# The last batch's u transposed by transfers, batch 0's state kept in PSUM, and a new order: a gated linear attention with a token and channel mixer on one core

## The chip, the cores and the metric

The kernel runs on one core of one Trainium2 chip, in one launch. The metric is the device time of that core in microseconds, as the median of several runs; lower is better. The core has a matrix engine (TensorE, PE in the profile), a vector engine (VectorE, DVE), an activation engine (ScalarE, ACT), a general engine (GpSimd, POOL) and a queue engine (SyncE, SP). Each works through its own list of instructions in order and waits on semaphores for what the others make.

## The reference

The inputs are q, k, v and f_logit, each of shape (4 batches, 8 heads, 768 steps, 48), and four weights. A gated linear attention is followed by a mixer over tokens and one over channels:

```python
def _attn_ref(q, k, v, f_logit):
    f = 1.0 / (1.0 + np.exp(-f_logit))
    state = zeros((B, H, D, D))
    for t in range(S):
        state = f[:, :, t, :, None] * state + einsum('bhd,bhe->bhde', k[:, :, t], v[:, :, t])
        y[:, :, t] = einsum('bhd,bhde->bhe', q[:, :, t], state)
    return y

def _moe_ref(x, w_tok1, w_tok2, w_ch1, w_ch2):      # x: (4, 768, 384), the heads side by side
    xt = x.transpose(0, 2, 1)
    h = np.maximum(xt @ w_tok1, 0.0) @ w_tok2       # w_tok1 (768, 256), w_tok2 (256, 768)
    u = x + h.transpose(0, 2, 1)
    h2 = np.maximum(u @ w_ch1, 0.0) @ w_ch2         # w_ch1 (384, 1536), w_ch2 (1536, 384)
    return u + h2
```

## The kernel before

**Tiling.** Each batch's 768 steps are cut into six chunks of 128. Within a chunk the recurrence is computed as a masked product of q and k times v, and between chunks a state is carried.

**The stages of a chunk.** `gates` makes the logarithm of the gate (ACT) and its low half (DVE or POOL). `sums_and_turns` adds these up along the chunk on PE, takes exponentials on ACT (`GG`), scales q and k with them on DVE (`qk`, L586) and transposes both: on PE with a copy out of PSUM (L603) for batches 0 to 2, and by a transposing transfer issued from SP (L593) for batch 3 (`TURNED = 3`). `attention` computes the scores (L504) and the chunk's part of the state (L520, `parts`) on PE. `rest` masks the scores (`AmT`, L640), updates the state, copies it in two halves into the bf16 tile `state_bd`, and computes the chunk's output y on PE from `state_bd` of the chunk before (L671) and from the masked scores (L678).

**The state.** It lies in SBUF. For the first chunk it is the part scaled by the decay `glast` (L649); for each later chunk the part, which stands in a PSUM bank of its own, is first added to it (`tsum`, L652) and the sum is scaled (L654).

**The mixer.** Two products over the tokens (`tok1` L708, `tok2` L724) give u; u is cast to bf16 (`u_bf`) and transposed in two halves of three tiles (nine 128x128 blocks each) on PE (L765), with three copies by DVE or ACT per half (`uT`). The first channel product (`ch1`, L783) is 24 groups of three matmuls per batch, whose results go through a relu on ACT or DVE into `zT`; the second (`ch2`, L802) is six groups of 12 matmuls, whose results are added to u on DVE (L808) and written out from SP (L812). The code has a branch already that transposes u by two transfers; `U_TURNED` lists the batches that take it and is empty.

**The order.** The kernel first collects all its work as operations of a `Plan`: for each the engines that may do it, a rank, what it needs and makes, a PSUM bank, and a duration. `Plan.order` then runs a list schedule over these: it takes the operation that can start first by its durations (plus a lag of its own), and on a tie the one of lowest rank. The instructions are issued in the order that comes out, so the plan's durations and landing times decide each engine's order, while the chip decides the times. `SHIFTS` holds, for some of the operations by number, a rank and a lag that override the written ones. `LATE` adds some hundred nanoseconds to the plan's landing time of batch 0's loads. Where the plan sees PE idle in the first 25.5 us, it puts filler matmuls on the constant tile `steady` (L849).

**The loads.** Batch 0's q, k, v come one chunk at a time from POOL's queue, f_logit from SP's; then the weights and the later batches from POOL's.

Of the kernel before, what the change touches and what calls it, by code (L numbers as in the profile page):

```python
# [19 lines left out]
U_TURNED = ()  # L20
TURNED = 3
SHIFTS = (
# [860 lines left out]
```

## Time and profile before

| what | us |
|---|---|
| median of 3 runs | 178.74 |
| lowest and highest run | 178.43, 179.81 |
| span of the profiled execution | 176.5 |
| PE busy in it | 165.9 (94%) |
| DVE, ACT, POOL busy in it | 127.1, 120.3, 100.9 |

The span is the time from the first to the last instruction of the one profiled execution. No time of that execution as a run is listed beside its span; the runs' median lies 2.24 us above the span. Busy time of PE counts its filler matmuls, and the durations of matmuls overlap, because they are pipelined. In the profile's rows a line number is that of the kernel before; several operations can share a line where a helper issues them (`copy_on` is L459 on ACT, L461 on DVE, L463 on POOL). In a row of the timeline the first number is the start, the second the time taken, x the number of instructions merged; brackets give the idle time before it and what ended it.

### The profile page before, as it was taken

How to read it: one execution, taken by the hardware profiler on the slowest of the kernel's cores; microseconds unless marked ns; L12 is line 12 of the kernel's file. 1: busy time of each engine (PE TensorE's matmuls, PEld its weight loads, DVE VectorE, ACT ScalarE, POOL GpSimd, SP SyncE). 2: the span in 40 equal slices, each digit the busy share in tenths (PEclk: the TensorE clock that was granted, in tenths of full speed). 3: DMA queues.
4: the chain of work that ended last, by engine and by line, in shares of the span. 5: the costliest groups of instructions: out<-in, count | busy, mean ns of one | idle time of the engine just before them, and what ended most of it. 6: DMA issues, size and time to landing. Idle time of an engine off the chain costs nothing.

```text
span 176.5 us, 4283 instructions
## 1 busy us (share of the span) xinstructions
PE 165.9 (94%) x1649; PEld 104.7 (59%) x1653; DVE 127.1 (72%) x286; ACT 120.3 (68%) x273; POOL 100.9 (57%) x136
## 2 busy tenths in 40 slices
PE   6898898899999999799999999999999999999991
PEld 2355565556666676466567666675667666655660
DVE  6469886996888999988959995899485566401321
ACT  4688895879599676999897789847844332795000
POOL 7999568994499978987994997602011120000000
PEclk9999999999999999999999999999999999999998
DMA  7999999999999999999998999943902011200232
GB/s 101 131 159 161 138 169 180 214 151 204 186 168 141 225 233 97 199 116 92 113 160 45 121 193 147 202 104 59 123 9 85 2 45 49 90 0 0 87 106 78
DMA packets 97796, 21.54 MB, mean 122 GB/s; under 512 B 90512, under 2 KB 96912, under 8 KB 97776
## 3 DMA queue, kind: packets, MB, share of 16 engines
q0 software_dynamic: 79440, 13.77, 98.0%
q1 hardware_dynamic: 18336, 7.51, 19.0%
q8 instruction: 13, 0.21, 0.5%
q14 instruction: 7, 0.06, 0.1%
HBM read 25.17 MB, written 4.72 MB: 169 GB/s over the span
## 4 chain that ended last, share of the span: by engine, by line
PE 51%; ACT 5%; DVE 3%; issue 0%
PE ps L802 20%; PE ps L783 17%; PE ps L708 2%; PE ps L724 2%; PE ps L504 2%; PE ps L765 1%; ACT u_bf L459 1%; DVE AmT L640 1%; PE ps L678 1%; PE ps L603 1%; PE ps L520 1%; PE ps L671 1%; PE ps L554 1%; DVE x_nat L808 1%; PE ps L555 1%; ACT ends L574 1%
## 5 line engine op out<-in xcount | busy, mean ns | idle before, releaser
L802 PE MATMUL ps<-w_ch,zT 128*128 128x384 bf16 (+2 forms) x300 | 52.4, 320 | 0.0
L783 PE MATMUL ps<-uT,w_ch 128*128 128x384 bf16 x288 | 51.9, 326 | 0.4 <-ACT zT L468 0.4
L468 ACT ACTIVATE zT<-ps 128x384 bf16<-128x384 f32 x70 | 33.3, 491 | 14.8 <-PE ps L783 12.5
L802 PEld LDWEIGHTS <-zT 128*128 128x128 bf16 x300 | 27.7, 98 | 16.6
L783 PEld LDWEIGHTS <-w_ch 128*128 128x128 bf16 x288 | 27.2, 98 | 17.4 <-issue 0.9
L640 DVE TENSOR_TENSOR AmT<-ps,tri_bf 128x512 bf16<-128x512 f32 x46 | 29.9, 682 | 3.6 <-PE ps L504 3.4
L401 POOL DMA_DIRECT2D v_sb<-in_v_dram x24 | 22.4, 933 | 4.4 <-DMA w_ch<-in_moe_w_ch_dram 4.4
L808 DVE TENSOR_TENSOR x_nat<-x_nat,ps 128x384 f32<-128x384 f32 (+2 forms) x25 | 13.3, 535 | 16.1 <-PE ps L802 15.9
L401 POOL DMA_DIRECT2D qk_sb<-in_k_dram x24 | 22.7, 947 | 0.8 <-POOLq L867 0.8
L401 POOL DMA_DIRECT2D qk_sb<-in_q_dram x24 | 22.7, 946 | 0.0
L470 DVE TENSOR_SCALAR zT<-ps 128x384 bf16<-128x384 f32 x26 | 13.8, 550 | 8.4 <-PE ps L783 8.4
L586 DVE TENSOR_TENSOR qk<-qk_sb,GG 128x768 bf16<-128x768 bf16 (+1 forms) x30 | 14.2, 479 | 4.7 <-ACT GG L565 2.2
L463 POOL CAST state_bd<-state 48x192 bf16<-48x192 f32 x13 | 4.4, 342 | 21.8 <-DVE state L654 11.4
L401 POOL DMA_DIRECT2D f_sb<-in_f_logit_dram x18 | 16.6, 947 | 0.2
L479 ACT ACTIVATE f_sb<-f_sb 128x384 f32<-128x384 f32 x24 | 12.4, 516 | 3.5 <-DMA f_sb<-in_f_logit_dram 3.3
L849 PE MATMUL ps<-steady 128*128 128x512 bf16 x37 | 11.6, 431 | 1.6 <-DVE steady L433 1.5
L459 ACT ACTIVATE state_bd<-state 48x192 bf16<-48x192 f32 x27 | 9.7, 360 | 4.4 <-DVE state L654 3.5
L565 ACT ACTIVATE GG<-ps 128x384 bf16<-128x384 f32 x24 | 11.6, 487 | 1.6 <-PE ps L555 1.4
L603 PE MATMUL ps<-ident,qk 128*128 128x128 bf16 x144 | 11.4, 220 | 1.0 <-DVE qk L586 0.9
L567 ACT ACTIVATE GG<-ps 128x384 bf16<-128x384 f32 x24 | 11.3, 493 | 0.6 <-PE ps L555 0.3
L603 PEld LDWEIGHTS <-qk 128*128 128x128 bf16 x144 | 8.8, 98 | 4.6 <-DVE qk L586 3.1
L740 DVE TENSOR_TENSOR x_nat<-x_nat,ps 128x384 f32<-128x384 f32 x21 | 10.5, 546 | 0.8 <-PE ps L724 0.7
(75 smaller groups left out, 245.6 us busy)
## 6 DMA issues: line engine op xcount, KB each, us to landing
out_dram<-x_nat SPq DMA_DIRECT2D x23, 192.0 KB, 3.1
f_sb<-in_f_logit_dram POOLq DMA_DIRECT2D x18, 192.0 KB, 5.4
qk_sb<-in_k_dram POOLq DMA_DIRECT2D x24, 96.0 KB, 5.2
qk_sb<-in_q_dram POOLq DMA_DIRECT2D x24, 96.0 KB, 5.3
v_sb<-in_v_dram POOLq DMA_DIRECT2D x24, 96.0 KB, 5.2
f_sb<-in_f_logit_dram SPq DMA_DIRECT2D x6, 192.0 KB, 4.3
w_ch<-in_moe_w_ch_dram POOLq DMA_DIRECT2D x2, 576.0 KB, 7.2
w_ch<-in_moe_w_ch_dram POOLq DMA_DIRECT2D x1, 1152.0 KB, 11.3
```

The source lines that it names most:

```text
L401: lambda eng=eng, into=into, of=of: eng.dma_start(out=into, in_=of),
L468: nc.scalar.activation(out_, in_, AF.Relu, bias=0.0, scale=1.0)
L470: nc.vector.tensor_scalar(out_, in_, 0.0, None, ALU.max)
L479: add(ACT, r, lambda: nc.scalar.activation(fb, fb, AF.Exp, bias=0.0, scale=-1.0), make=[key], kind=el)
L565: add(ACT, r, lambda: nc.scalar.activation(G[i], sview(), AF.Exp, bias=0.0, scale=-1.0), make=[("G", i)], bank=p_s, kind=el)
L586: add(DVE, r, lambda n=n: nc.vector.tensor_tensor(qk[i4][:, n, :, 0:D], qk_sb[nb][:, n, :, c, :], GG[i][:, n], ALU.mult), need=[(x, nb, c) ...
L603: nc.tensor.transpose(to[:, o + hp, :], blk(src)[:, hp, :], ident)
L640: add(DVE, r, lambda half=half, made=made: nc.vector.tensor_tensor(half, made(), tb4, ALU.mult), need=["tri_bf"], make=[("AmT", i, p)], ba ...
L783: nc.tensor.matmul(banks[pm.at][:, 0:384], lhsT=w[:, kt, c0:c0 + 128], rhs=uT[:, th, :, kt, :], start=(kt == 0), stop=(kt == 2))
L802: nc.tensor.matmul(banks[pm.at][:, 0:n1 - n0], lhsT=zT[:, kt, tt * 128:(tt + 1) * 128], rhs=w_ch2[:, kt, n0:n1], start=(kt == 0), stop=(kt ...
L808: add(DVE, rank("ch2", tt), lambda un=un, pm=pm, n=n1 - n0: nc.vector.tensor_tensor(un, un, banks[pm.at][:, 0:n], ALU.add), make=[("x_nat" ...
L849: nc.tensor.matmul(banks[NBANK - 1], lhsT=steady[:, 0:128], rhs=steady, start=True, stop=True)
```

## The change

It has four parts.

1. `U_TURNED = (3,)`: the last batch's u is transposed by two transfers issued from SP, each of which waits for three tiles of `u_bf` and writes one half of `uT`. The 18 PE transposes and six copies of that batch go.
2. Batch 0's state stays in one PSUM bank, `p_st`. The matmuls of `parts` add onto it, DVE scales it in place, and the two copies to `state_bd` read it there, on ACT or DVE. `tsum` and the SBUF state are used from batch 1 on only. `parts` of batch 0 is now an operation of its own, no longer tied to the scores in front of it.
3. The plan takes the landings of batch 0's q, k, v and of the two token weights from a table of times (`SLOTS`), and those of f_logit from a table of delays (`HELD`), in place of `LATE`.
4. `SHIFTS` is a new table, which gives nearly all of the 1125 operations a rank and a lag.

```diff
-U_TURNED = ()
+U_TURNED = (3,)
 TURNED = 3
 SHIFTS = (
-    (8,-60,3900), (38,-50,3700), (42,-50,3800), (48,-50,3800), (53,50,3400), (55,300,6300), (85,0,2500),
...
+    (0,-34375,1200), (1,-34428,700), (2,-34357,0), (3,-34277,0), (4,-34359,0), (5,-32498,2200),
...
-LATE = {("f", 0, 1): 900, ("f", 0, 2): 200, ("f", 0, 3): 600, ("f", 0, 4): 700, ("f", 0, 5): 900,
...
+SLOTS = (4700, 6200, 7400, 8250, 10000, 11000, 11750, 12850, 13900, 14650, 15850, 16950, 17800, 18550, 19250,
+         19950, 20650, 21500, 23700, 26450)
+HELD = (0, 4400, 4450, 4200, 4600, 5400)
...
-                if len(op.kind) > 5:
-                    op.end += op.kind[5]
+                if e == POOL and size and op.kind[4] > 8000 or slot in (18, 19) and size and e == POOL:
+                    op.end = max(t + 3500, SLOTS[slot])
+                    wire = op.end - 1100
+                    slot += 1
+                elif op.kind[5:] and op.kind[5]:
+                    op.end = t + op.kind[5]
...
+    p_st = Bank()
+
     def attention(b, cs, due):
...
-        p_d, live = Bank(), [c for c in cs if c < NCH - 1]
+        p_d, live = p_st if b == 0 else Bank(), [c for c in cs if c < NCH - 1]
...
-        if live:
-            chain = add(PE, due(b, cs[0]), lambda: None, need=need, bank=p_d, kind=("mm", 1),
-                        room=1 if b == 0 else 3)
+        if live and b:
+            chain = add(PE, due(b, cs[0]), lambda: None, need=need, bank=p_d, kind=("mm", 1), room=3)
...
-                                     rhs=v_sb[nb][:, h, c, :], start=True, stop=True)
-
-        if live:
+                                     rhs=v_sb[nb][:, h, c, :], start=b > 0 or (c == 0 and hp == 0), stop=True,
+                                     skip_group_check=b == 0)
+
+        if live and b == 0:
+            add(PE, due(b, cs[0]), parts, need=[("kh", cs[0] % 4), ("v", nb, cs[0])], make=["sums"], bank=p_d,
+                kind=("mm", 345, 238))
+        elif live:
...
-            if c == 0:
+            if b == 0:
+                add(DVE, r, lambda: nc.vector.tensor_tensor(dg(), dg(), gb, ALU.mult),
+                    need=[("glast", g4)], make=["sums"], bank=p_d, kind=small)
+            elif c == 0:
...
-                op = add(((POOL, ACT) if c > 2 else ACT, ACT, (ACT, POOL), POOL)[b], r, None, need=["state", ("sbd", i)], make=[("sbd", i, cols.start)],
-                         kind=("el", HP * D, False, 1))
+                op = add(((ACT, DVE), ACT, (ACT, POOL), POOL)[b], r, None,
+                         need=["state" if b else "sums", ("sbd", i)], make=[("sbd", i, cols.start)],
+                         kind=("el", HP * D, b == 0, 1), bank=None if b else p_d)
                 op.fn = lambda op=op, rows=rows, cols=cols: copy_on(
-                    op.engine, state_bd[i][rows, :, cols], state[rows])
+                    op.engine, state_bd[i][rows, :, cols], state[rows] if b else dg()[rows])
```

The branch that part 1 turns on is in the kernel before (`op` durations of 1500, 5000 and 1900 ns are the plan's: SP's own time, the time to landing, and the share of the transfers' engines):

```python
        for th in range(2 if b in U_TURNED else 0):
            add(SP, rank("ut", 3 * th), lambda th=th: nc.sync.dma_start_transpose(
                out=uT[:, th].rearrange("p tt d t -> p (tt d) t"),
                in_=u_bf[:, 3 * th:3 * th + 3, :].rearrange("t tt n -> t (tt n)")),
                need=[("u_bf", 3 * th + j) for j in range(3)],
                make=[("uT", 3 * th + j, d) for j in range(3) for d in range(3)], kind=("fix", 1500, 5000, 1900))
```

More of the change, by code (lines that the diff above doesn't have):

```diff
@@ L208, in order @@
         banks = [0.0] * (NBANK - 1) + [until]
-        wire = 0.0
+        wire, slot = 0.0, 0
         landed: list = []
@@ L402, in load @@
                 make=[(n, i, j) for j in range(cs.start, cs.stop)],
-                kind=("load", 430 if engine == SP else 900,
-                      128 * H, size, 8000 if b else 20000, LATE.get((n, b, c), 0)))
+                kind=("load", 430 if engine == SP else 900, 128 * H, size, 8000 if b else 20000,
+                      *(() if b else (HELD[c] if engine == SP else -1,))))
     def load_w(name, dst, src, size):
@@ L509, in attention @@
             chain = add(PE, due(b, cs[0]), lambda c=c, k=k: scores(c % 4, heads[k]), need=need, bank=heads[k][1],
-                        kind=("mm", own if live else own + 107, own), tail_of=chain)
+                        kind=("mm", own if live and b else own + 107, own), tail_of=chain)
             plan.maker[heads[k][0]] = chain
```

234 rows, old and new, of tables (LATE, SHIFTS) are left out of this document.

## The prediction

> **What bounds the kernel now.** I read the stretches of the span first, cut where the first and the last channel matmuls begin and end, then the chain that ended last, then the timeline of the first 35 us and of the last batch, and the waits.
>
> ```profile
> core 0: us, PE busy (x) PEld busy (x) DVE busy (x) ACT busy (x) POOL busy (x), PEclk, DMA share, GB/s
> 0.00:34.16 34.16, 29.08 (x336) 16.88 (x341) 25.98 (x75) 25.00 (x60) 28.91 (x46) 1.00 1.62 157
> 34.16:146.85 112.69, 110.73 (x1140) 71.69 (x1138) 92.98 (x195) 84.25 (x191) 71.94 (x91) 1.00 1.31 127
> 146.85:172.94 26.09, 26.05 (x179) 16.18 (x176) 7.55 (x18) 11.08 (x23) 0.00 (x0) 1.00 0.17 62
> 172.94:176.50 3.56, 0.00 (x0) 0.00 (x0) 0.55 (x1) 0.00 (x0) 0.00 (x0) 0.86 0.15 55
> ...
> L849 PE MATMUL ps<-steady 128*128 128x512 bf16 x37 | 11.6, 431 | 1.6 <-DVE steady L433 1.5
> ```
>
> From 34.16, where batch 0's first channel matmul starts, to 172.94, PE is idle for 112.69 - 110.73 = 1.96 us and 26.09 - 26.05 = 0.04 us, at full granted clock. So 138.8 us of the 176.5 are bought with PE work alone: there, only a removed matmul or one of those 2.0 us can shorten the end. The first 34.16 us are different: PE is idle for 34.16 - 29.08 = 5.08 us, and 11.6 us of what counts as busy are 37 filler matmuls on a constant tile (the durations overlap). There the landings of batch 0 and the latency behind them set the pace. The last 3.56 us are one addition and the last output transfer; no edit touches them.
>
> ```profile
> 145.54 0.50 PE ps L765 x9
> ...
> 150.92 0.50 PE ps L765 x9
> 151.42 9.75 PE ps L783 x60
> ...
> 172.94 0.55 DVE x_nat L808
> ```
>
> This is the chain of waits near its end: nothing but PE from the last batch's transposes on. The two groups of nine transposes of u are the ones the change takes away.
>
> **Part 1, the last batch's u.** Removed: 18 PE transposes, 2 x 0.50 = 1.00 us of the chain, and six DVE copies of 0.346 us. Added: two transposing transfers on SP, each of 9 blocks of 128x128, and PE's wait for them. The trace has their like: the six transposes of q and k of this batch, 8 blocks each.
>
> ```profile
> L593 SPq DMA_TRANSPOSE qkT<-qk x6: 1232/1257/1351, 105.4 to 125.3; - x6
> DMA to landing us min/median/max: 3.1/3.7/5.5
> ...
> 105.39 1.35 SPq L593 DMA_TRANSPOSE qkT<-qk  x1
> qkT<-qk SPq DMA_TRANSPOSE x1, 5.5
> ...
> L461 DVE COPY uT<-ps x6: 345/346/357, 145.7 to 152.4; 128x384 bf16<-128x384 bf16 x6
> ...
> SPq L812 <- DVE x_nat L808: 53.1, 18, 11.9
> ...
> 145.19 0.51 POOL L463 CAST u_bf<-x_nat 128x384 bf16<-128x384 f32 x1 [0.89 <-DVE x_nat L740]
> 145.38 0.67 PE L765 MATMUL ps<-ident,u_bf 128*128 128x128 bf16 x9
> ...
> 146.20 0.81 PE L802 MATMUL ps<-w_ch,zT 128*128 128x384 bf16 x4
> 146.85 1.63 PE L783 MATMUL ps<-uT,w_ch 128*128 128x384 bf16 x9
> 148.31 1.46 PE L802 MATMUL ps<-w_ch,zT 128*128 128x384 bf16 x8
> 149.62 0.65 PE L783 MATMUL ps<-uT,w_ch 128*128 128x384 bf16 x3
> 150.10 0.81 PE L802 MATMUL ps<-w_ch,zT 128*128 128x384 bf16 x4
> 150.75 0.67 PE L765 MATMUL ps<-ident,u_bf 128*128 128x128 bf16 x9
> ```
>
> A transfer waits for three casts of u; the third ends at 145.19 + 0.51 = 145.70. Scaled by 9/8, the landing takes 3.7 x 9/8 = 4.2 us (estimate; from 3.1 and 5.5: 3.5 to 6.2). The first channel matmul of the batch would then start at 149.9, not 146.85: 3.05 us later. What can fill this on PE is batch 2's second channel product, of which 12 matmuls still stand behind 146.85 (8 + 4, 1.30 + 0.65 = 1.95 us in the chain). So with all else as it is, 1.1 us would be exposed and the 1.0 us saved would be given back; with the slowest landing 3.1 us would be exposed (5.05 - 1.95), net +2.1; with more of batch 2 held back nothing is, net -1.0. The second half is cheap: its transfer lands behind 36 channel matmuls of the first half, 36 x 0.1625 = 5.9 us of cover (9.75 us / 60 each). More filler exists: four more of these matmuls run at 146.20, and others earlier, between the token products, whose waits they cover. The diff gives the transfer 5000 ns in the plan, more than the 4.2 I expect, so the new order should hold back enough. I take -0.8 (0.2 us left exposed), with -1.0 and +2.1 as ends. On SP the two issues of 1.26 us are queued among the output transfers, and an output that waits (18 times for a sum on DVE, up to 11.9 us) holds a transpose placed behind it; what is queued behind the transposes is outputs alone, which nobody waits for until the end. The freed 2.1 us of DVE lie beside PE work and I count them as nothing: DVE is busy 7.55 of 26.09 us in that stretch.
>
> A rule speaks against this part: the Trainium skill, "VectorE: DVE Perf Modes", section "The three transpose paths", gives a 128x128 bf16 block 390 ns on TensorE and 1309 ns by the transposing transfer, and its rules say to use TensorE. By that price nine blocks would take 11.8 us (estimate) and the part would lose some 7 us. The trace does not agree: eight blocks landed 3.1 to 5.5 us after issue, not 10.5, so they are not done one after another at that price.
>
> **Part 2, batch 0's state in PSUM.** Removed: four additions (tsum) on DVE. Kept: the scaling, now in place in the bank, and two copies per chunk, now read from PSUM, by ACT or DVE; POOL can no longer take the two that it had.
>
> ```profile
> L652 DVE TENSOR_TENSOR tsum<-state,ps x4: 341/341/347, 14.7 to 26.0; 128x192 f32<-128x192 f32 x4
> L649 DVE TENSOR_TENSOR state<-ps,glast x1: 348/348/348, 13.3 to 13.3; 128x192 f32<-128x192 f32 x1
> L459 ACT ACTIVATE state_bd<-state x8: 347/360/363, 13.7 to 27.3; 48x192 bf16<-48x192 f32 x8
> L463 POOL CAST state_bd<-state x2: 336/340/345, 23.8 to 24.2; 48x192 bf16<-48x192 f32 x2
> ...
> 15.00:20.00 5.00, 3.90 (x56) 2.35 (x57) 4.39 (x13) 4.63 (x13) 4.79 (x7) 1.00 2.39 152
> 20.00:25.00 5.00, 4.80 (x82) 3.46 (x81) 4.60 (x14) 4.30 (x12) 2.25 (x5) 1.00 1.72 173
> ```
>
> DVE loses 4 x 0.341 = 1.36 us, ACT and DVE gain about 2 x 0.35 = 0.70 us; together -0.66 us on two engines that are 4.4 to 4.6 of 5 us busy just where the scan runs. A copy from PSUM of this shape isn't in the trace; the scaling of the same 192 columns reads PSUM in 0.348 and the ACT copy reads SBUF in 0.360, so I take no difference. There is a new wait: a chunk's part of the state may be added only after the scaling and both copies of the chunk before (0.35 + 2 x 0.36 = 1.07 us when both are on ACT), and in PE's order the transposes and scores placed behind it wait too; DVE and ACT wait for those. Before, the part went to a bank of its own and the adding waited on DVE. The chain per chunk is as long as it was (matmul, scaling, copies instead of addition, scaling, copies). One bank of the eight is held through the scan, instead of one from a chunk's scores to its addition. Ends: -1.36 (all of the removed work on the path) and +1.07 (the new wait once, not covered). I take -0.2, a third of the -0.66, since half of those engines' work there waits on landings.
>
> **Part 3, the landings in the plan and the order.** These move work only. How much the start can give is bounded by when batch 0's last data land.
>
> ```profile
> 1.32 1.05 POOL L401 DMA_DIRECT2D qk_sb<-in_k_dram  x1 [0.80 <-POOLq L867]
> qk_sb<-in_k_dram POOLq DMA_DIRECT2D x1, 96.0 KB, 4.6
> ...
> 16.04 0.96 POOL L401 DMA_DIRECT2D qk_sb<-in_k_dram  x1
> qk_sb<-in_k_dram POOLq DMA_DIRECT2D x1, 96.0 KB, 6.3
> 16.91 0.96 POOL L401 DMA_DIRECT2D qk_sb<-in_q_dram  x1
> qk_sb<-in_q_dram POOLq DMA_DIRECT2D x1, 96.0 KB, 5.8
> 24.29 0.73 DVE L586 TENSOR_TENSOR qk<-qk_sb,GG 128x384 bf16<-128x384 bf16 x2
> ...
> 19.78 0.70 POOL L408 DMA_DIRECT2D w_tok<-in_moe_w_tok_dram  x1 [0.21 <-issue]
> w_tok<-in_moe_w_tok_dram POOLq DMA_DIRECT2D x1, 384.0 KB, 7.8
> 30.33 2.11 PE L724 MATMUL ps<-h1T,w_tok 128*128 128x384 bf16 x12 [0.49 <-DVE h1T L470]
> ```
>
> The last chunk's k lands at 16.04 + 6.3 = 22.34 and its q at 16.91 + 5.8 = 22.71, and they are first used at 24.29 and 24.66: 1.95 us of slack. The second token weight lands at 19.78 + 7.8 = 27.58 and is used at 30.33: 2.75 us. The queue of loads is not reordered, so the start can give at most 1.95 us. Against the whole of it: the diff's table puts this k at 19.95 and q at 20.65 of the plan's clock, 2.39 and 2.06 us ahead of the trace, while the first k (4.70 in the table, landed at 1.32 + 4.6 = 5.92) is 1.22 ahead; so the plan counts on the last chunk about 1 us too early and the engines, which run in order, will wait there. I take -0.8, with -1.95 and +1.0 (the wait with no gain) as ends. In the middle a search can win back at most the 1.96 us of idle time and can lose any of it again; I take -0.4, with -1.96 and +4 as ends (twice the present idle time more; the least certain number here).
>
> **The sum.** -0.8 - 0.2 - 0.8 - 0.4 = -2.2 us on the profiled execution's span of 176.5 us: 174.3. The runs' median, 178.74, is 2.24 us above that span; I carry this over, since nothing around the span changes: 176.5 us, 1.2% faster. A change of about 1% (1.8 us) is what a measurement of this kernel tells from none.
>
> **The rivals.**
> - All parts pay in full: -1.0 for u, -1.95 for the start, -1.9 in the middle: 173.9 us. For it: PE is idle or filling for much of the first 34 us. Against: the plan's early landings and DVE and ACT near full there.
> - The transposes are hidden anyway, or paid back: 1.1 us exposed for 1.0 saved, the start and the middle unchanged, since the order was near PE's work already: 178.8 us. For it: the 12 matmuls of cover as they stand, and 98% of busy PE in the middle. Against: a plan that knows the 5 us.
> - The last batch's transposed u comes late (the slower side). Place: PE before the first channel matmul of batch 3. The transfer takes 6.2 us from the slowest row, or stands on SP behind an output that waits. Price: 3.1 exposed - 1.0 saved = 2.1 us; with nothing gained elsewhere 180.8 us. It decides from a stall of about 1.0 us on, where the part begins to lose. Against: the 5.5 us landing was of the transfer issued at 105.39, beside loads; from 146.85 on the queues move 62 GB/s against the 127 of the stretch before.
> - The newly searched order stalls PE in the middle. Place: between 34 and 147 us, where one early instruction in PE's queue holds all behind it. Price: 4 us more idle, less the 0.8 and 1.0 gained for u and the start (with part 2): 180.9 us. Against: the old order lost only 1.96 us by the same method.
>
> **How the numbers follow.** The forecast gets 0.44, with a range of its own from 175.3 to 177.4 (parts 1 and 3 shifted by about 1 us either way); three quarters of it lie below 176.95, the 1% bound. In full 0.12; paid back 0.20 (0.17 within 1%, 0.03 above); late u 0.12; stalls in the middle 0.12. Faster by over 1%: 0.33 + 0.12 = 0.45. Within 1%: 0.11 + 0.17 = 0.28. Slower: 0.03 + 0.12 + 0.12 = 0.27. The range reaches from the full payment to the two slower cases, 173.7 to 181.0; less than 0.2 is left outside, mostly above.
>
> **What would show it.** Right: no PE transposes of u in the last batch, and less than 0.5 us of PE idle before its first channel matmul; first channel matmul of batch 0 about 1 us earlier than 34.16; PE idle from there to the last matmul not above 2 us; no tsum before 35 us. Wrong: the transfers landing more than 5 us after issue or issued late behind an output; the last chunk's q and k still first used at 24 us; more than 3 us of PE idle between the first and the last channel matmul.

## The result and the profile after

The kernel after takes 176.42 us (median of 4 runs, 175.93 to 176.76) against 178.76 us for the kernel before beside it: a ratio of 0.9856, 95% interval 0.9828 to 0.9885. The same kernel in a second comparison gave 176.47 us and 0.9857 [0.9811, 0.9903]. The forecast was 176.5.

The profiled execution of after spans 174.9 us; before's spanned 176.5. That pair understates the change: each run lists its span, and their medians are 174.55 (after) and 176.8 to 177.3 (before, in three comparisons), so the profile of before was one of its shortest executions and that of after one of its longer ones. In all these runs the time is some 1.7 us above the span.

The stretches of the span of after, cut at the same places as those of before (first channel matmul of batch 0, first channel matmul of the last batch, end of the last matmul):

```profile
core 0: us, PE busy (x) PEld busy (x) DVE busy (x) ACT busy (x) POOL busy (x), PEclk, DMA share, GB/s
0.00:34.34 34.34, 27.88 (x328) 16.03 (x329) 26.15 (x74) 24.39 (x59) 27.98 (x43) 1.00 1.63 156
34.34:148.23 113.89, 111.90 (x1143) 72.38 (x1141) 90.03 (x184) 87.25 (x196) 74.84 (x96) 1.00 1.31 130
148.23:171.82 23.59, 23.59 (x158) 14.61 (x155) 9.61 (x19) 6.68 (x14) 0.00 (x0) 1.00 0.18 68
171.82:174.90 3.08, 0.01 (x1) 0.00 (x0) 0.30 (x2) 0.00 (x0) 0.00 (x0) 1.00 0.38 131
```

From the first channel matmul to the last matmul PE is busy 111.90 + 23.59 = 135.49 us, against 136.78 before: 1.29 us less work. Its idle time there is 1.99 us, against 2.00: nothing won back, nothing lost. The start is no shorter in these two profiles (34.34 against 34.16). One profile of each is a weak measure of it, though: in the four kernels below that share before's start (b_dma_u, b_dma_cov, b_tail, b_tail2) the first channel matmul stands at 34.27 to 34.78, in three that share after's (a_again, a_pe_u, a_u23) at 33.51 to 34.64. The tail, which no part of the change was meant to touch, is 3.08 us instead of 3.56.

The last batch's u, in the timelines of PE and of SP of after:

```profile
144.01 0.49 PE L840 MATMUL ps<-h1T,w_tok 128*128 128x384 bf16 x2
144.33 4.06 PE L918 MATMUL ps<-w_ch,zT 128*128 128x384 bf16 x24
148.23 1.95 PE L899 MATMUL ps<-uT,w_ch 128*128 128x384 bf16 x11
```

```profile
143.08 3.95 SPq L870 DMA_TRANSPOSE uT<-u_bf  x2
```

and in the view of the tile `uT`, its two rows on the transfers (ns; the second in us):

```profile
L870 SPq DMA_TRANSPOSE uT<-u_bf x2: 1290/1292/1295, 143.1 to 145.7; - x2
DMA to landing us min/median/max: 2.8/2.9/2.9
```

The first transfer is issued at 143.08 and has landed by 143.08 + 2.9 = 146.0. PE has 24 matmuls of batch 2's second channel product to do from 144.33 on, twice the 12 that stood there before, and goes over to the first channel matmul at 148.23 without a wait: 2.2 us of cover to spare.

The start of after, from the timeline of PE (brackets: idle time before, and what ended it):

```profile
30.03 2.11 PE L840 MATMUL ps<-h1T,w_tok 128*128 128x384 bf16 x12 [0.49 <-DVE h1T L578]
31.97 0.28 PE L881 MATMUL ps<-ident,u_bf 128*128 128x128 bf16 x2
32.72 0.56 PE L881 MATMUL ps<-ident,u_bf 128*128 128x128 bf16 x7 [0.47 <-ACT u_bf L567]
33.83 0.68 PE L881 MATMUL ps<-ident,u_bf 128*128 128x128 bf16 x9 [0.54 <-DVE u_bf L856]
34.34 0.98 PE L899 MATMUL ps<-uT,w_ch 128*128 128x384 bf16 x5
```

### The profile page after: what moved, and what is told of

It is laid out like the page before. It is cut to its first block, busy times and chain, and to the rows that moved or that the text cites. A ratio compares the mean times of both kernels' runs of the same rounds, so it can differ in the third digit from the quotient of the medians.

```text
span 174.9 us, 4237 instructions
## 1 busy us (share of the span) xinstructions
PE 163.4 (93%) x1624; PEld 103.0 (59%) x1624; DVE 126.1 (72%) x278; ACT 118.3 (68%) x268; POOL 102.8 (59%) x139
## 4 chain that ended last, share of the span: by engine, by line
PE 73%; ACT 8%; POOL 6%; DVE 4%; DMA 4%; issue 2%; DVEq 0%; POOLq 0%
PE ps L899 27%; PE ps L918 25%; DMA qk_sb<-in_q_dram 4%; POOL qk_sb L509 3%; PE ps L840 3%; PE ps L715 3%; PE ps L824 3%; PE ps L612 3%; PE ps L794 2%; PE ps L787 2%; ACT u_bf L567 2%; PE ps L666 2%; PE ps L667 1%; POOL v_sb L509 1%; ACT state_bd L567 1%
## 5 line engine op out<-in xcount | busy, mean ns | idle before, releaser
L918 PE MATMUL ps<-w_ch,zT 128*128 128x384 bf16 (+2 forms) x300 | 51.6, 320 | 0.2 <-ACT zT L576 0.2
L899 PE MATMUL ps<-uT,w_ch 128*128 128x384 bf16 x288 | 50.8, 326 | 0.0
L576 ACT ACTIVATE zT<-ps 128x384 bf16<-128x384 f32 x69 | 32.8, 490 | 15.4 <-PE ps L899 15.2
L571 POOL CAST state_bd<-state 48x192 bf16<-48x192 f32 x14 | 5.1, 363 | 12.3 <-DVE state L769 10.6
L677 ACT ACTIVATE GG<-ps 128x384 bf16<-128x384 f32 x24 | 11.6, 486 | 1.1 <-PE ps L667 0.9
L567 ACT ACTIVATE x_bf<-ps 128x384 bf16<-128x384 f32 x16 | 7.8, 489 | 5.7 <-PE ps L794 4.9
L965 PE MATMUL ps<-steady 128*128 128x512 bf16 x30 | 9.8, 444 | 1.5 <-DVE steady L541 1.5
```

The lines of the kernel that those rows point to most:

```text
L567: nc.scalar.activation(out_, in_, AF.Copy, bias=0.0, scale=1.0)
L576: nc.scalar.activation(out_, in_, AF.Relu, bias=0.0, scale=1.0)
L899: nc.tensor.matmul(banks[pm.at][:, 0:384], lhsT=w[:, kt, c0:c0 + 128], rhs=uT[:, th, :, kt, :], start=(kt == 0), stop=(kt == 2))
L918: nc.tensor.matmul(banks[pm.at][:, 0:n1 - n0], lhsT=zT[:, kt, tt * 128:(tt + 1) * 128], rhs=w_ch2[:, kt, n0:n1], start=(kt == 0), stop=(kt ...
```

## The experiments

### Undoing one part at a time

Three kernels keep after's order of all other instructions. In a_pe_u the last batch's u is transposed on PE again; in a_sbuf batch 0's state lies in SBUF again, with its four additions and with copies that read SBUF; a_order has both undone, so that the order and the plan alone remain of the change.

```diff
 # a_pe_u: at the place of each of the two transfers' plan operations
+    nc.tensor.transpose(to[:, j * 128:(j + 1) * 128], u_bf[:, 3 * th + j, d * 128:(d + 1) * 128], ident)   # nine
+    nc.vector.tensor_copy(uT[:, th, :, d, :], ...)                                                         # three
 # a_sbuf: in batch 0, in place of the scaling in PSUM
-    nc.vector.tensor_tensor(dg(), dg(), gb, ALU.mult)
+    if c:
+        nc.vector.tensor_tensor(tsum, state, dg(), ALU.add)
+    nc.vector.tensor_tensor(state, tsum if c else dg(), gb, ALU.mult)
```

> The changed kernel, its order kept, with the last batch's u turned on PE again: 18 transposes and six copies put back where the casts of u are ready, the two transfers left out. Theory (PE is the bound from the first channel matmul on, and the transfers are hidden): PE has 1.0 us more to do, so 177.4 us against 176.4, and the last batch's first channel matmul starts about 1.0 us later than 148.2. Rival (the gain is the order's alone, the transposes lay in idle time): 176.4. Rival (each transpose costs its row's 0.219 us): 18 x 0.219 = 3.9 us more, 180.3.

> The changed kernel, its order kept, with batch 0's state in SBUF again: each scaling is preceded by the addition (tsum), and the copies read SBUF. Theory (the start is set by when the data land, and DVE and ACT have slack there): 176.4 to 176.6. Rival (DVE is the bound of the start): four additions of 0.34 us more on the path, 177.8.

> Both edits undone in the changed kernel's order: u on PE and the state in SBUF, so that against the kernel before only the order and the plan's landings are changed. Theory (the transposes give 1.0, the order the rest): 177.4 to 177.6, 1.2 us below the kernel before. Rival (the order gives nothing): 178.7. Rival (the order gives all): 176.4.

| kernel | median us | ratio to before | first channel matmul | PE busy from there | tail |
|---|---|---|---|---|---|
| before, beside them | 178.62 | 1 | 34.16 | 136.77 | 3.61 |
| a_order | 177.88 | 0.9968 [0.9948, 0.9987] | 34.47 | 136.45 | 3.20 |
| a_pe_u | 177.19 | 0.9921 [0.9891, 0.9951] | 34.56 | 136.44 | 3.22 |
| a_sbuf | 176.91 | 0.9899 [0.9874, 0.9924] | 34.54 | 135.60 | 3.05 |
| after | 176.42 | 0.9856 [0.9828, 0.9885] | 34.34 | 135.49 | 3.08 |

(The last three columns are from one profiled execution each; those of before and after are the ones shown above, measured to the end of the last matmul, 172.89 in before. The profile of a_pe_u is of its slowest run.) Beside each other on one chip, the order and the plan are worth 178.62 - 177.88 = 0.7 us, the transfers 177.88 - 176.91 = 1.0 us and the state in PSUM 177.88 - 177.19 = 0.7 us. The sum, 2.4, is the 2.3 that the whole change gained, so the parts add up. Each is uncertain by about 0.5 us. Of the expectations, that of a_pe_u came out (177.19 for 177.4); a_order lies 0.3 us above its 177.4 to 177.6, and a_sbuf between its theory (176.4 to 176.6) and its rival (177.8). The gain of the transfers can be seen in the profile: PE's work after the first channel matmul falls by 136.44 - 135.49 = 0.95 us. That of the state cannot be seen there (136.45 and 136.44, 135.60 and 135.49), so it should come from the start. These profiles do not show it there: after's start ends between 33.51 and 34.64 from one execution to the next, which is more than the gain.

### The transfers alone, in before's order

In b_dma_u the kernel before keeps its order, and only the 18 transposes and six copies of the last batch give way to two transfers behind the third cast of each half. b_dma_cov also moves the 12 matmuls of batch 2's second channel product ahead of the first channel matmul of batch 3.

```diff
+    nc.sync.dma_start_transpose(out=uT[:, th]..., in_=u_bf[:, 3 * th:3 * th + 3, :]...)   # behind the third cast of a half
 # b_dma_cov too:
+    ahead((888, 889, 884), 1107)     # three groups of four ch2 matmuls ahead of the first ch1 group
```

> The kernel before, its order kept, with the last batch's u turned by two transfers, each issued where the third cast of its half is; the 18 PE transposes and their copies are left out. No other work is moved, so the matmuls that would cover the transfer stay behind the first channel matmul. Theory (the transfer's landing decides where its cover is missing): the third cast of the first half ends at 145.2, the landing takes 2.9 us as in the changed kernel, so PE waits from about 146.3 to 148.3, 1.9 us, and has 1.0 us less to do: 179.5, 0.9 above the kernel before. Rival (the prediction's 4.2 us landing): 3.1 us of waiting, 180.7. Rival (transfers are free wherever they stand): 177.6.

> As the run before, but 12 matmuls of batch 2's second channel product (1.95 us) are moved ahead of the last batch's first channel matmul. Theory (what counts is the work held back, not the transfer): the wait shrinks from 1.9 us to 0.1 and the run is about 1.0 us below the kernel before, 177.6 to 177.8. Rival (4.2 us landing): 1.2 us of waiting stay, 178.8.

b_dma_u took 180.31 us, ratio 1.0104 [1.0065, 1.0142]; b_dma_cov 178.83 us, 0.9977 [0.9945, 1.0008]; before beside them 179.12. PE's timeline of b_dma_u, and the landing in its view of `uT`:

```profile
145.81 0.81 PE L802 MATMUL ps<-w_ch,zT 128*128 128x384 bf16 x4
149.07 1.62 PE L783 MATMUL ps<-uT,w_ch 128*128 128x384 bf16 x9 [2.45 <-DMA uT<-u_bf]
```

```profile
DMA to landing us min/median/max: 2.8/3.0/3.2
```

The same two views of b_dma_cov:

```profile
146.15 2.76 PE L802 MATMUL ps<-w_ch,zT 128*128 128x384 bf16 x16
149.19 3.07 PE L783 MATMUL ps<-uT,w_ch 128*128 128x384 bf16 x16 [0.29 <-DMA uT<-u_bf]
```

```profile
DMA to landing us min/median/max: 2.8/2.9/3.0
```

So the same edit loses 1.2 us where only four matmuls stand behind the transfer. Where 12 more do, it comes out 0.3 us under before, which the interval doesn't tell from none. PE waits 2.45 us in the one and 0.29 in the other, and the landing hardly differs. (In b_dma_u the wait was expected to be 1.9 us, with a third cast that ends at 145.2; SP issued the first transfer at 145.81.) What after adds to the edit is an order in which 24 matmuls stand there.

### What sets the start: the landings of the loads?

The plan of after counts on landings 1 to 2.6 us earlier than they come (below), and the chain that ended last goes back to them. If that is what holds the start, a delay of POOL's loads must come out at the end in full. a_late puts a store of zeros ahead of POOL's first load; a_again is after unchanged, beside it; a_late2 has a longer store.

```diff
-    add(POOL, -20.0, lambda: None, kind=("load", 600, 600, 0))
+    add(POOL, -20.0, lambda: nc.gpsimd.memset(zT.rearrange("p a b -> p (a b)")[:, 0:700], 0.0), ...)   # a_late2: 0:1900
```

> The changed kernel with a memset of about 0.7 to 1.0 us on POOL ahead of its first load, so that all of POOL's loads of batch 0 land that much later; the order is unchanged. Theory (the start hangs on the landings): the first channel matmul and the end move by as much as the first load's issue, 177.2 to 177.5. Rival (the start is bound by DVE and ACT, with slack behind the landings): less than 0.3 us, 176.7 at most.

> The changed kernel once more, beside the others on this chip, for a second profile and more times. Theory (two profiles of the same kernel differ mainly in when the loads land): 176.4, and a first channel matmul that differs from the first profile's 34.34 by up to 0.5 us while the stretch from it to PE's end stays at 137.5. Rival (the profiles differ everywhere): that stretch differs as well.

The first channel matmul of a_again stands at 34.64, 0.30 us later, within what was expected. The stretch from it to PE's end is 137.79 us, not 137.5: two executions of one kernel differ behind the start too, by 0.3 us here.

a_late told nothing: 176.48 us, 0.9850 [0.9807, 0.9892], beside 176.47 for a_again. POOL stood idle for 0.8 us ahead of its first load, the store (0.68 us) fitted into that, and the load moved by 0.1 us only.

> The kernel after, with a longer store of zeros on POOL (128 x 1900 bf16 into zT, which is written again long before it is read) ahead of the first load that POOL issues. The shorter one moved that issue by only 0.1 us; this one should move it by 1 to 1.5 us. Theory: the first 34 us are set by the landings of POOL's loads, so everything from the first token matmul on moves by nearly as much as the first load's issue: first channel matmul and span later by 0.8 to 1.5 us, time 177.3 to 178.0 (after 176.4). Rival 1: the start is set by the work on PE, DVE and ACT and its chain of waits, and the landings have slack: time within 0.3 us of after, 176.2 to 176.8. Rival 2: in between, some landings count and some don't: +0.3 to +0.8.

a_late2 took 177.63 us, 0.9936 [0.9915, 0.9958]. POOL's first load and the first channel matmul in the timeline, after first, then a_late2:

```profile
1.32 1.01 POOL L509 DMA_DIRECT2D qk_sb<-in_k_dram  x1 [0.80 <-POOLq L983]
```

```profile
2.43 1.01 POOL L509 DMA_DIRECT2D qk_sb<-in_k_dram  x1
35.36 1.95 PE L900 MATMUL ps<-uT,w_ch 128*128 128x384 bf16 x11
```

The loads go out 1.11 us later, the first channel matmul begins 1.02 us later than 34.34, and the time is up by 177.63 - 176.47 = 1.16 us. Two things blur this. The two times are from different chips; against before beside each (0.9936 and 0.9857) the difference is 1.4 us. And three of the nine runs, the profiled one among them, show a mean granted clock of 0.988 to 0.990 and take 177.7 to 178.0 us; the other six have a median of 177.1, 0.6 us above a_again. In the profile the clock stands at 0.50 from 11 to 14 us (last section). It did so in a_pe_u's profile too, whose first channel matmul came at 34.56 all the same, so the half clock by itself does not explain 1.02 us. The rival by which the landings have slack (within 0.3 us) falls; the one by which some landings count and some don't (0.3 to 0.8) is not ruled out. The store also holds up the masks and the identity that POOL makes between its loads, so this is the whole of POOL's start moved, not the loads alone.

### What the state in PSUM frees: VectorE in the start

> The kernel after with batch 0's state in SBUF again (as in the run that undid this part: ratio 0.9899, 176.9 us) and with each of the four additions of two head pairs' sums written twice, so four more VectorE operations of about 0.36 us, 1.4 us in all, in the stretch ahead of 34 us. Theory: VectorE's time in the start counts in full or by half because its queue stands on the way from batch 0's state to the first token matmuls: the first channel matmul later by 0.6 to 1.4 us, time 177.5 to 178.3. Rival: the start waits for loads and VectorE's additions lie in those waits: time 176.7 to 177.2, and then what the PSUM state gained came from elsewhere.

```diff
     if c:
         nc.vector.tensor_tensor(tsum, state, dg(), ALU.add)
+        nc.vector.tensor_tensor(tsum, state, dg(), ALU.add)
```

a_sbuf_x2 took 178.23 us, 0.9974 [0.9955, 0.9993], 1.3 us more than a_sbuf's 176.91: the four added operations (4 x 0.346 = 1.38 us by its rows) count in full as far as can be told: the two were measured on different chips, each beside before, and the difference is uncertain by some 0.5 us. Its first channel matmul stands at 35.59, 1.05 us behind a_sbuf's. Taking four such additions away gained 0.5 to 0.7 us, about half. The stretch of the scan, 12 to 26 us, and who VectorE waited for in it, suggest why. First a_sbuf, its stretch and VectorE's one wait there (total us, times, longest):

```profile
12.00:26.00 14.00, 11.16 (x182) 7.26 (x182) 13.37 (x35) 12.14 (x31) 9.59 (x13) 1.00 2.09 162
```

```profile
DVE qkT L569 <- PE ps L714: 0.2, 1, 0.2
```

The same two views of after:

```profile
12.00:26.00 14.00, 11.75 (x184) 7.44 (x184) 12.28 (x31) 11.89 (x31) 9.68 (x13) 1.00 2.04 163
```

```profile
DVE qk L698 <- DMA qk_sb<-in_q_dram: 0.8, 2, 0.5
DVE qkT L569 <- PE ps L715: 0.6, 1, 0.6
```

With the state in SBUF, DVE is busy for 13.37 of 14 us and waits for no load: it is the bound there, and a microsecond added to it came out as a microsecond at the end. With the state in PSUM it is busy for 12.28 us and waits 0.8 us for q to land: the bound has passed in part to the loads, and some of the saving is spent in that wait. The chains that ended last point the same way. Up to 26 us the last landing on them ends at 5.6 us in a_sbuf, 11.1 in a_order and 12.3 in a_sbuf_x2, but at 18.6, 19.5 and 19.1 in after, a_again and a_late, where it is each time the q issued at 11.6 to 11.8. (a_pe_u, whose clock was halved for a while, is an exception with 8.2.)

The four additions are not all that a_sbuf changes in DVE's work. DVE also makes two of the ten copies to `state_bd`, and these differ (from the view of that tile: after, a_sbuf, a_sbuf_x2):

```profile
L569 DVE CAST state_bd<-ps x2: 349/350/350, 9.4 to 18.0; 48x192 bf16<-48x192 f32 x2
```

```profile
L569 DVE CAST state_bd<-state x2: 737/738/739, 9.3 to 18.1; 48x192 bf16<-48x192 f32 x2
```

```profile
L569 DVE CAST state_bd<-state x2: 251/252/253, 9.2 to 18.9; 48x192 bf16<-48x192 f32 x2
```

From PSUM a copy took 0.35 us in every profile; from SBUF it took 0.25 or 0.74 (in a_order one of each kind, 0.25 and 0.79). Why was not tested. So part of the 1.09 us between 13.37 and 12.28 is one slow copy, and the steps of 1.3 and of 0.5 to 0.7 us hold more than four additions.

### The tail

In after the last thing to be added and stored is the 96-column piece of the split output tile; in before it is a full tile of 384 columns. b_tail and b_tail2 move matmuls of before's last output tiles in this direction.

```diff
 # b_tail
+    ahead((1124, 1125, 1126), 1134); ahead((1127, 1128), 1137)                       # the last full tile ahead of the wide piece
 # b_tail2
+    ahead((1124, 1125, 1126), 1139); ahead((1129, 1130, 1131, 1134, 1135, 1136), 1139)
+    ahead((1127, 1128, 1132, 1133, 1137, 1138), 1142)                                # the 96-column piece last
```

> The kernel before with one move at the very end: the last full output tile's 12 matmuls, addition and transfer go ahead of the second half of the split tile, so that the last piece is 128x288 instead of 128x384, as in the changed kernel the last pieces are the split tile's. Theory (half a microsecond of the gain is the shorter last addition and transfer): 178.3, 0.4 to 0.5 below the kernel before, with the stretch from PE's last matmul to the end about 3.1 to 3.3 us instead of 3.6. Rival (the last transfer takes the same whatever its size): 178.6, only the addition's 0.1 us.

> The kernel before, with the second channel matmuls of the last output tiles in another order, so that the 96-column piece of the split tile is the last to be added and stored (as in the kernel after), and the last full tile goes ahead. Theory: the end behind the last matmul is as long as the last piece's addition and transfer: 3.1 us behind the last matmul instead of 3.6, as after, and the time 0.4 to 0.5 us under before, ratio about 0.9975. Rival: what ends the kernel is the sum of the transfers still under way, whatever the last one's size: tail 3.5 to 3.6, ratio 0.999 to 1.001.

Neither moved the time: 178.62 us, 0.9997 [0.9978, 1.0016], and 178.69 us, 1.0007 [0.9987, 1.0027]. b_tail left the wide piece last, with a tail of 3.52 us; b_tail2 has the 96-column piece last, yet a tail of 177.0 - 173.28 = 3.72 us. The transfers that SP issues last, in the timeline: before, after, b_tail2.

```profile
173.52 0.33 SPq L812 DMA_DIRECT2D out_dram<-x_nat  x1
```

```profile
171.89 0.81 SPq L928 DMA_DIRECT2D out_dram<-x_nat  x2
```

```profile
173.36 1.31 SPq L812 DMA_DIRECT2D out_dram<-x_nat  x3
```

In b_tail2 three issues stand one behind another after the last matmul (173.28), and the last ends at 174.67, 1.39 us behind it; in after two, ending 0.88 us behind (172.70 against 171.82); in before one, of a full tile, 0.96 us behind. From there to the end of the span it is 2.33 us in b_tail2, 2.20 in after and 2.65 in before: the small piece ends sooner by 0.3 to 0.45 us, and in b_tail2 the queue of issues takes that back. So a small last piece alone gains nothing when other issues queue ahead of it. That after's shorter tail is worth 0.4 us in the runs was not shown by itself; it is seen in the profiles of all the kernels with after's order (2.92 to 3.22 us).

### The same trade one batch earlier

> The kernel after, with batch 2's u turned by two transfers too: 18 PE transposes and 6 VectorE copies around 112 to 118 us go; SP issues the two transfers ahead of a transfer of qk at 111.4 and ahead of an output store at 116.2, and four groups of channel matmuls of the first half go ahead of the second half's. Theory: the same gain as in batch 3 where cover stands behind it, PE has 1.0 us less to do, the landing of 2.9 us ends within 0.6 us of PE's need, and the time is 0.5 to 1.0 us under after: 175.4 to 176.0. Rival: in this stretch SP's queue also carries the transfers of qk and the gates' ends, and each lies 1.3 us later; attention of the next pairs waits, or the transfer lands in 4 to 5 us among the loads: time 176.4 to 178.

```diff
 # the 18 transposes and six copies of batch 2's u are left out; SP gets, ahead of a transfer of qk and of an output store:
+    nc.sync.dma_start_transpose(out=uT[:, th]..., in_=u_bf[:, 3 * th:3 * th + 3, :]...)
+    ahead((805, 807, 813, 811), 851)     # four ch1 groups of the first half ahead of the second half's
```

(The groups moved ahead write two PSUM banks that still hold attention products of batch 3; that part is not computed as in the reference, and the run is read for its times and waits alone.) It took 184.16 us, 1.0277 [1.0231, 1.0324]; 7.7 us above after (on another chip; 7.5 by the ratios), and worse than the rival's 178. PE's waits for the transfers of u:

```profile
PE ps L899 <- DMA uT<-u_bf: 5.2, 2, 3.8
```

The two added transfers in the view of `uT`, and the second of them in that of the DMA issues:

```profile
L975 SPq DMA_TRANSPOSE uT<-u_bf x2: 1988/2090/2192, 110.7 to 116.9; - x2
```

```profile
uT<-u_bf SPq DMA_TRANSPOSE x1, 7.5
```

The stretches ahead of, in and behind the longer wait:

```profile
117.00:120.70 3.70, 3.48 (x47) 2.10 (x46) 1.76 (x3) 0.98 (x3) 3.70 (x5) 1.00 1.48 126
120.70:124.50 3.80, 0.00 (x0) 0.00 (x0) 1.44 (x4) 0.00 (x0) 0.93 (x3) 0.86 1.96 170
124.50:130.00 5.50, 5.49 (x18) 2.55 (x18) 0.00 (x0) 2.45 (x5) 0.00 (x0) 0.50 1.05 83
```

Beside POOL's loads for the next stage (POOL is busy issuing them for 3.70 of 3.70 us) the transfers take 2.0 to 2.2 us to issue and 4.1 and 7.5 us to land, where the last batch's take 1.3 and 2.9 us. Whether the loads make them late, or the transposes of qk that SP issues just before and behind each of them, was not separated. PE then waits 5.2 us, and that is not all of the price: after its pause of 3.8 us it is granted half of its clock, and 18 matmuls take 5.49 us. PE's busy time from the first channel matmul on is 138.16 us, 2.67 more than in after in spite of 18 transposes fewer. The runs agree: one of the six has a mean granted clock of 1.000 and took 181.64 us; the other five, at 0.981 to 0.991, took 183.6 to 184.6.

## Why the prediction was right, step by step

**The sum.** 176.5 forecast, 176.42 measured. The mechanism of part 1 was right; the terms for the state (too small) and for the start and the middle (too large, and in the wrong place) were each off by up to half a microsecond, and they cancelled. That the sum came within 0.1 us is luck.

| step | forecast us | measured us | by |
|---|---|---|---|
| u by transfers | -0.8 | -1.0 (-0.95 of PE work) | a_order to a_sbuf; a_pe_u to after |
| state in PSUM | -0.2 | -0.5 to -0.7 | a_sbuf to after; a_order to a_pe_u |
| start and middle by the order | -0.8 and -0.4 | -0.7 with the tail's share | before to a_order |
| outside the span | +2.24 | +1.7, and 0.5 by which before's profile was short | the spans of before's and after's runs |

**Part 1: right in mechanism, the landing too long.** The forecast was 4.2 us, scaled by 9/8 from eight blocks; nine blocks landed in 2.8 to 3.2 us in after, b_dma_u and b_dma_cov. Even the quickest of the scaled rows, 3.1, gives 3.5, so the step by 9/8 has no support here; the rows were also in part taken beside loads, while the transfers of u run when POOL has none left. Which of the two made the estimate long is open. The first channel matmul without the 12 matmuls as cover was reckoned 3.05 us late, and 1.1 us with them; it came 2.22 us late (149.07 against 146.85, after a wait of 2.45) in b_dma_u, and after a wait of 0.29 in b_dma_cov. The trade of "1.0 us saved against what is exposed" holds roughly: 2.45 - 1.0 = 1.4 by it and 1.2 measured; 0.29 - 1.0 = -0.7 by it and -0.3 measured, with an interval of half a microsecond either way. And the plan did hold back more of batch 2's matmuls, 24 instead of 12. The rival of a late transfer did not come true here, but a_u23 shows it one batch earlier, at a price well above the 2.1 us that was put on it: the landing was longer than the 6.2 us assumed and a slower clock follows the wait.

By the price that the Trainium skill, "VectorE: DVE Perf Modes", section "The three transpose paths", gives for one 128x128 block by a transfer (1309 ns), nine blocks would take 11.8 us (estimate). The trace does not agree, neither with 2.9 us in the last batch nor with 7.5 us in a_u23.

**Part 2: the term too small.** -0.2 was reckoned as a third of 0.66 us, "since half of those engines' work there waits on landings". That clause is the step that failed. The trace of before speaks against it already: from 12 to 26 us its DVE is busy 12.83 of 14 us, and its longest wait there is for ACT, none for a load.

```profile
12.00:26.00 14.00, 12.51 (x203) 8.41 (x202) 12.83 (x33) 12.45 (x33) 11.04 (x16) 1.00 2.00 161
```

```profile
DVE Llo L485 <- ACT L L480: 0.6, 1, 0.6
```

With the state in SBUF, DVE in after's order waits for no landing either, so its work counts (a_sbuf_x2), until the landings become a bound too. The prediction also took copies from PSUM and SBUF as equal; DVE's were not, as shown above. The feared new wait of PE's order on the scaling and both copies did not appear among PE's longer waits.

**Part 3: the place was wrong.** 0.8 us were expected from the start; the order alone gained nothing there that the profiles show (34.47 in a_order, against 34.16 to 34.78 in five profiles with before's start). The first channel matmul did not come about 1 us earlier, as the prediction asked for; its other signs (no wait ahead of the last batch's first channel matmul, not more than 2 us of idle time behind the start, no tsum in it) hold. The objection that the prediction itself raised, that the plan counts on the last chunk too early, was borne out and should have set the value. In after, POOL's timeline and the view of the DMA issues give for the last q:

```profile
16.83 0.97 POOL L509 DMA_DIRECT2D qk_sb<-in_q_dram  x1
```

```profile
qk_sb<-in_q_dram POOLq DMA_DIRECT2D x1, 96.0 KB, 6.4
```

and the chain that ended last has an earlier q:

```profile
11.60 6.98 DMA qk_sb<-in_q_dram
```

The last q lands at 16.83 + 6.4 = 23.23, 2.58 us behind the 20.65 of the table, while the first k, at 1.32 + 4.3 = 5.62, is 0.92 us behind its 4.70: the table falls behind by another 1.7 us on the way. The chain runs through the landing of the fourth chunk's q (7.0 us), and DVE waits for that one and the next. The slack of 1.95 us that was read in before's trace is slack of the last chunk alone. In after DVE reaches that chunk 0.6 us earlier (23.67 against 24.29), still about 1 us after the landing of its k (15.96 + 6.7 = 22.66); the landings that hold it up are earlier ones, whose slack the prediction did not read. What the order did gain, 0.7 us, lies in the profiles behind the start: 0.3 us less PE time (136.77 to 136.45, with 1317 matmuls in both; why was not found) and the shorter tail (3.61 to 3.20).

**The middle** gained none of the 0.4: PE is idle for 1.99 us as before. The rival of a stall there did not come true either.

**The tail.** "No edit touches them", of the last 3.56 us, was wrong, because the new order also chose which output piece comes last.

**The remainder of 2.24 us** was 1.7 us plus a profile of before that was half a microsecond shorter than its median. Carried over whole, it put the sum back on the median run, so the forecast of the change did not suffer; with 1.7 us on that short span it would have come out near 176.0.

## What to carry to other kernels

Work may be moved from the bounding engine to a transfer where the landing has cover of its own length, counted in instructions that really stand there: the same edit was worth -1.0, -0.3 (not clear of noise), +1.2 and over +7 us, by what stood behind it and what else was in flight. Slack at one landing says nothing of the ones before it: here DVE, nearly always busy, hid them, and with its work shortened earlier landings held it up. Do not read a start from one profile when it varies by 1 us between executions. Compare the span of the one profiled execution with the median span of the runs before taking half a microsecond from it.

## What the runs showed of the hardware

A pause of PE of 3.8 us cost more than itself: the granted clock was 0.50 for the 5.5 us after it (a_u23), while a pause of 2.45 us left it at 1.00 in the profiled execution of b_dma_u, whose stretch behind the wait follows.

```profile
146.00:149.10 3.10, 0.65 (x5) 0.29 (x4) 1.57 (x3) 1.04 (x2) 0.00 (x0) 1.00 0.67 161
149.10:156.00 6.90, 6.90 (x43) 4.17 (x43) 2.13 (x4) 3.22 (x7) 0.00 (x0) 1.00 0.36 102
```

The Trainium skill, "TensorE: Matmul & The Clock Gate", section "HAM oscillation — how this bites in real kernels", warns of idle gaps of PE above about 3.4 us, behind which it starts again at half clock. The two pauses lie on the two sides of that figure, but the figure does not settle it here. Four of the 12 runs of b_dma_u have a mean granted clock of 0.991 and take 181.5 to 182.5 us; the other eight, at 0.999 to 1.000, take 180.05 to 180.43. And in two profiles, a_pe_u and a_late2, the clock fell to 0.50 from 11 to 14 us with no wait of PE above 0.61 us in the 5 us before. These are the stretches of a_late2, then of after:

```profile
8.00:11.00 3.00, 1.91 (x28) 1.07 (x29) 2.04 (x7) 2.54 (x7) 3.00 (x5) 1.00 1.57 100
11.00:14.00 3.00, 2.78 (x19) 1.54 (x21) 1.89 (x4) 0.74 (x2) 3.00 (x7) 0.50 2.28 163
```

```profile
8.00:11.00 3.00, 2.16 (x28) 1.11 (x27) 2.19 (x6) 2.74 (x8) 3.00 (x6) 1.00 1.53 119
11.00:14.00 3.00, 2.83 (x44) 1.72 (x43) 2.60 (x7) 1.72 (x6) 3.00 (x5) 1.00 2.30 168
```

From 8 to 11 us PE was busy 1.91 us in a_late2 and 1.47 in a_pe_u, against 2.16 in after, which kept its clock. So a long wait is not needed for it; how little work is too little, these runs do not show.

The issue of one transposing transfer of u on SP took 1.25 to 1.35 us in the last batch, with no load of POOL's beside it, and 2.0 to 2.2 us in a_u23, beside loads and other transposes; its landing 2.8 to 3.2 us against 4.1 and 7.5 us.
